# An S5 state-space layer and a feed-forward layer, mixed by a gate: paired 64-row remainders, D·x of odd tokens on GpSimd, one rotation of PSUM banks

## The chip, the cores and the metric

One core of one Trainium2 chip. The time is device microseconds (us) of one launch, as the median of several runs; a run of this kernel differs from the next by up to about 1.6%. "Span" is the time from the first to the last instruction in the one profiled run; it is 1.7 to 2.0 us shorter than that run's launch. The engines are TensorE (PE in the profile, its weight loads PEld), VectorE (DVE), ScalarE (ACT), GpSimd (POOL) and SyncE (SP), which here only issues transfers.

## The reference, cut to what matters

```python
# x: [1, 2048, 448]; P = D = 448; F = 1792; all inputs bf16
g = sigmoid((x * gate_w).sum(-1, keepdims=True))         # one gate per token
# A: a diagonal linear recurrence over the 2048 tokens, complex state of 448
h_t = Lam_bar * h_{t-1} + B_bar @ x_t
a   = 2 * real(C @ h_t) + x * Dskip                      # "D*x" below is x * Dskip
# B: feed-forward
b   = silu(x @ w1) @ w2                                  # 448 -> 1792 -> 448
out = g * a + (1 - g) * b
```

The kernel treats tokens as 1024 pairs. Even and odd tokens go through FFN1 (x @ w1) and FFN2 (@ w2) as separate chunks of 512 tokens, so there are four chunks: two even ones, then two odd ones. The recurrence is run over pairs, with tables of sines and cosines that ScalarE makes (`tables`), a projection on TensorE (`bu`), scans on VectorE (`scan`), combinations of C on VectorE (`side_C`, giving CO and CE), and at the end the y tiles on TensorE (`ytile`). `k0` is the small product of C and B that the even y tiles need.

## The kernel before: the parts that matter

A helper records every operation with the buffers that it reads and writes, and puts in the waits. An operation on an engine thus waits for the last writer of what it reads and for the readers of what it overwrites.

FFN1 contracts over 448 rows, which is three and a half blocks of 128. The half block is padded with zeros to 128 rows, so a block of 128 hidden units costs four matmuls of 512 columns:

```python
BK_F1 = [0, 1, 2, 3]              # PSUM banks of FFN1
BK_F2 = BK_S = [4, 5, 6, 7]       # PSUM banks of everything else

def ffn1(c, fb, ...):             # c: chunk, fb: one of 14 blocks of hidden units
    ...
    for j in range(4):
        ins = pe.matmul(ps[:, bank, :], W[:, j, fb*128:(fb+1)*128],
                        XT[:, j0 + j, h*512:(h+1)*512], start=(j == 0), stop=(j == 3))
    ...
    act: AT[:, fb, :] = Silu(ps[:, bank, :])
```

In an even y tile D·x is folded into `k0`. In an odd one it is four small matmuls with diagonal matrices DO:

```python
def ytile(kt, odd):
    for m in range(7):
        pe.matmul(ps[:, bank, 0:D], HS[:, m, o0:o0+128], C[:, m, :], start=(m == 0), stop=False)
    if odd:
        ...                       # four matmuls of 64 or 128 columns with DO
    else:
        ...                       # four matmuls with KT (from k0)
    dve: out = ps * GT1 + bs(tile)          # g * a + (1-g) * b
```

The gates, on VectorE, read x in its natural layout (XN, which lies where the odd w1 goes later):

```python
def gate():
    for t in range(16):
        dve: JK = XN[:, t*D:(t+1)*D] * GWB, Z[:, t] = row sums    # two SBUF inputs
    ...
    act: GT0 = Tanh(0.5 * Z)
    dve: GT1, GT2 = 0.5 +- 0.5 * GT0
    sp:  load odd w1 into the place of XN
```

The order of the program from the middle on is: gates' sums, `bu` of the first states, `scan(0)`, more `bu`, Tanh, the rest of the scans, FFN2 of chunk 0, FFN1 of chunk 2, FFN2 of 1, C combinations, FFN1 of 3, FFN2 of 2, `k0`, then FFN2 of 3 between y tiles.

Of the kernel before, what the change touches and what calls it, by code (L numbers as in the profile page):

```python
# [10 lines left out]
F32 = DT.float32  # L11
# [133 lines left out]
def gated_mix(nc, A_x, A_Lambda_re, A_Lambda_im, A_B_re, A_B_im, A_C_re, A_C_im, A_log_dt,  # L145
              A_Dskip, B_x, B_w1, B_w2, gate_w, out):
    with ExitStack() as ctx:
# [22 lines left out]
        DO = sb("DO", [128, 4, 128], BF16)  # L170
# [13 lines left out]
        R = sb("R", [3, 512], BF16)  # L184
        RD = sb("RD", [2, 512], BF16)
        PV = sb("PV", [128, 4, 5], F32)
# [5 lines left out]

        LTF = LT[:, :, :, :].rearrange("p a b c -> p (a b c)")
# [5 lines left out]
        BK_F1 = [0, 1, 2, 3]  # L199
        BK_F2 = BK_S = [4, 5, 6, 7]  # L200
# [8 lines left out]

        T.op("dve", lambda e: e.memset(Q1[:, 0, 0:512], 0.0), writes=["Q10"])  # L210
# [3 lines left out]
        T.op("pool", lambda e: e.memset(RD[:, :], 0.0), writes=["RD0", "RD1"])  # L214
        gR, gRD, gB = T.group(), T.group(), T.group()
# [3 lines left out]

        ld("act", W1E[:, 0:3, 0:384], B_w1[0:384, 0:384].rearrange("(j p) f -> p j f", p=128), "W1Eb")  # L220
# [4 lines left out]
        ldt(XT[:, 0:4, 0:512], x2[0:512, 0:512], "XTe0")  # L225
        for i, v in enumerate((A_log_dt, A_Lambda_re, A_Lambda_im)):
            ld("sp", R[i:i + 1, 0:D], row(v), f"R{i}", gR)
# [7 lines left out]
        for h in range(2):  # L235
            ldt(XT[:, 4:7, h * 512:(h + 1) * 512], x2[h * 512:(h + 1) * 512, 512:896], f"XTo{h}")
        B_RAW = ["Bre", "Bim"]
# [8 lines left out]
        T.op("pool", lambda e: e.memset(W1E[64:128, 3, :], 0.0), writes=["W1Ez"])  # L246
# [3 lines left out]
        T.op("pool", lambda e: e.memset(KT[64:128, 3, :], 0.0), writes=["KTz"])  # L250
        SGN = ["SGa", "SGb"]
# [3 lines left out]
        n_f1 = [0]  # L255
        n_f2 = n_s = [0]

        def nxt(banks, n):
            b = banks[n[0] % len(banks)]
            n[0] += 1  # L260
            return b

        def ffn1(c, fb, mm_only=False, act_only=None):
            odd, h = c // 2, c % 2
            bank = nxt(BK_F1, n_f1) if act_only is None else act_only
            W, j0 = (W1O, 3) if odd else (W1E, 0)
            a = AT[c % 2]
            wk = (["W1Oa", "W1Ob", "W1Oz"] if odd else
                  ["W1Ez", "W1Ea", "W1Eb" if fb < 3 else "W1Ec" if fb < 7 else "W1Ed"])
            xk = [f"XTe{h}", f"XTo{h}"] if odd else [f"XTe{h}"]  # L270

            def mm(pe):
                ins = None
                for j in range(4):
                    ins = pe.matmul(ps[:, bank, :], W[:, j, fb * 128:(fb + 1) * 128],  # L275
                                    XT[:, j0 + j, h * 512:(h + 1) * 512],
                                    start=(j == 0), stop=(j == 3))
                return ins
            if act_only is None:
                T.op("pe", mm, reads=wk + xk, writes=[f"ps{bank}"])  # L280
            if mm_only:
                return bank
            T.op("act", lambda e: e.activation(a[:, fb, :], ps[:, bank, :], AF.Silu),  # L283
                 reads=[f"ps{bank}"], writes=[f"AT{c % 2}_{fb}"])

        T.op("dve", lambda e: e.tensor_copy(R[:, D:512], R[:, 384:448]), reads=["R0", "R1", "R2"],
             writes=["Rd"])

        def mm_cols(pe):
            ins = None  # L290
            for pt in range(4):
                ins = pe.matmul(ps[:, 6, pt * 8:pt * 8 + 3], R[0:3, pt * 128:(pt + 1) * 128],
                                ID[0:3, 0:3], start=True, stop=True)
            return ins
        def warm(n):
# [7 lines left out]
        warm(10)  # L303
        first = [ffn1(0, fb, mm_only=True) for fb in range(2)]
        T.op("pe", mm_cols, reads=["R0", "R1", "R2", "Rd", "ID"], writes=["ps6"])
        T.op("dve", lambda e: e.tensor_copy(
            PV[:, :, 0:3], ps[:, 6, 0:32].rearrange("p (t c) -> p t c", c=8)[:, :, 0:3]),
            reads=["ps6"], writes=["PV"])

# [61 lines left out]
        def phase(pt):  # L371
            return HS[:, 2 * pt:2 * pt + 2, :].rearrange("p a b -> p (a b)")[:, 0:2 * NK].bitcast(F32)

        def phases(pt):
            f2 = "f2s" if pt == 3 else "f2"
            X, RR = phase(pt), G[:, 1, :]
            T.op("dve", lambda e: e.tensor_scalar(X, IOTA[:, :], c1(f2, pt), None, ALU.mult),
# [6 lines left out]
        def tables(pt):  # L384
            X = phase(pt)
            T.op("act", lambda e: e.activation(SIN[:, pt, :], X, AF.Sin, scale=SIN_SCALE),
                 reads=[f"F{pt}"], writes=[f"SIN{pt}"])
            yield
            T.op("act", lambda e: e.activation(X, X, AF.Abs), reads=[f"F{pt}"], writes=[f"F{pt}"])
            yield  # L390
            T.op("act", lambda e: e.activation(COS[:, pt, :], X, AF.Sin, bias=HP[:, 0:1],
                                               scale=-SIN_SCALE),
                 reads=[f"F{pt}", "HP"], writes=[f"COS{pt}"])
            T.op("pool", lambda e: e.memset(HS[:, 2 * pt:2 * pt + 2, 0:8], 0.0),
                 writes=[f"F{pt}", f"HSz{pt}"])
            yield
# [96 lines left out]
        def side_diag():  # L493
            def mm(pe):
                ins = None
                for pt in range(4):
                    ins = pe.matmul(ps[:, 7, pt * 8:pt * 8 + 2], RD[0:2, pt * 128:(pt + 1) * 128],
                                    ID[0:2, 0:2], start=True, stop=True)
                return ins
            T.op("pe", mm, reads=["RD0", "RD1", "ID"], writes=["ps7"])  # L500
            T.op("dve", lambda e: e.tensor_copy(
                PV[:, :, 3:5], ps[:, 7, 0:32].rearrange("p (t c) -> p t c", c=8)[:, :, 0:2]),
                reads=["ps7"], writes=["PVD"])
            for j in range(4):
                T.op("dve", lambda e, j=j: e.tensor_scalar(
                    DE[:, j, :], ID[:, :], PV[:, j, 3:4], None, ALU.mult),
                    reads=["ID", "PVD"], writes=[f"DE{j}"])
                T.op("dve", lambda e, j=j: e.tensor_scalar(
                    DO[:, j, :], ID[:, :], PV[:, j, 4:5], None, ALU.mult),
                    reads=["ID", "PVD"], writes=[f"DO{j}"])  # L510
# [4 lines left out]
        def load_xn():  # L515
            ld("sp", XN.rearrange("p (k c) -> p k c", k=NKT), x2.rearrange("(k p) c -> p k c", p=128), "XN")

        def gate():
            for t in range(2 * NKT):
# [4 lines left out]
                if t % 4 == 3:  # L524
# [9 lines left out]
            T.op("pool", lambda e: e.memset(W1O[0:64, 0, :], 0.0), writes=["XN", "W1Oz"])  # L534
            T.dma("sp", lambda e: e.dma_start(W1O[64:128, 0, :], B_w1[0:64, :]), reads=["W1Oz"],
                  writes=["W1Oa"])
            T.dma("sp", lambda e: e.dma_start(
                W1O[:, 1:4, :], B_w1[64:448, :].rearrange("(j p) f -> p j f", p=128)),
                reads=["W1Oz"], writes=["W1Ob"])
# [3 lines left out]
        def ffn2(c, q):  # L543
# [4 lines left out]
            bank = nxt(BK_F2, n_f2)  # L548

            def mm(pe):  # L550
                ins = None
                for fb in range(NFB):
# [7 lines left out]
                 reads=[f"ps{bank}", "GT2"], writes=[f"BS{tile}"])  # L560

        def bu(m, h):
            pt = m // 2
            bank = nxt(BK_S, n_s)
# [12 lines left out]
        def k0(j):  # L577
            bank = nxt(BK_S, n_s)
# [73 lines left out]
        hs_all = [f"HS{m}" for m in range(7)] + [f"HSz{pt}" for pt in range(4)]  # L652

        def ytile(kt, odd):
            tile = 2 * kt + odd
            bank = nxt(BK_S, n_s)
# [4 lines left out]
            def mm(pe):  # L661
                ins = None
                for m in range(7):
                    ins = pe.matmul(ps[:, bank, 0:D], HS[:, m, o0:o0 + 128], C[:, m, :],  # L664
                                    start=(m == 0), stop=False)
                if odd:
                    pe.matmul(ps[:, bank, 0:64], XT[:, 3, t0:t0 + 128], DO[:, 0, 64:128],  # L667
                              start=False, stop=False)
                    for j in range(1, 4):
                        lo = 64 + (j - 1) * 128  # L670
                        ins = pe.matmul(ps[:, bank, lo:lo + 128], XT[:, 3 + j, t0:t0 + 128],  # L671
                                        DO[:, j, :], start=False, stop=(j == 3))
                else:
# [6 lines left out]
                 + [f"KT{j}" for j in range(4)] + ["KTz"] + [f"DO{j}" for j in range(4)],  # L680
# [4 lines left out]
                bs(tile), ALU.mult, ALU.add),  # L685
                reads=[f"ps{bank}", "GT1", f"BS{tile}"], writes=[f"OT{kt % 3}_{odd}"])
# [13 lines left out]
        ld("sp", GWB[:, :], row(gate_w).partition_broadcast(128).rearrange("p o n -> p (o n)"), "GW")  # L700
        load_xn()
# [8 lines left out]
        for fb in range(2):  # L710
            ffn1(0, fb, act_only=first[fb])
        for fb in range(2, NFB):
            ffn1(0, fb)
        tabs = chain(tables(0), tables(3), tables(1), tables(2))
        for fb in range(NFB):
            ffn1(1, fb)
# [3 lines left out]
        run(gates, 5)  # L720
        for h in range(2):
# [6 lines left out]
        bu(6, 1)  # L728
        s3 = scan(3)
# [5 lines left out]
        run(gates)  # L735
# [3 lines left out]
        ld("sp", RD[0:1, 0:D], row(A_Dskip), "RD0", gRD)  # L739
        ld("sp", RD[1:2, 64:512], row(A_Dskip), "RD1", gRD)  # L740
# [9 lines left out]
        for fb in range(NFB):  # L750
            ffn1(2, fb)
# [3 lines left out]
        for fb in range(NFB):  # L755
            ffn1(3, fb)
        for q in range(4):
            ffn2(2, q)
        for j in range(4):
            k0(j)  # L760
        for q in range(4):
            ffn2(3, q)
# [43 lines left out]
```

## Time and profile before

| | before |
|---|---|
| median of the first three runs | 161.76 us |
| span of the profiled run (which took 162.38 us) | 160.6 us |
| TensorE busy | 153.4 us (96%) |
| VectorE busy | 108.6 us (68%) |
| GpSimd busy | 7.3 us (5%) |
| TensorE unbroken | from 14.10 us to 157.5 us |
| last CO piece ready / `k0` starts | 111.39 us / 112.22 us |

From the page of the profile, part 4, the chain of work that ended last, by engine:

```profile
PE 92%; DMA 4%; ACT 2%; DVE 1%; issue 0%
```

TensorE bounds the kernel. But its second is close. These are lines of VectorE's timeline (start in us, duration in us, engine, source line, operation, output<-inputs, sizes, count; in brackets the idle time before it and what ended that): the first gate operations, the first operation of the scans, and the last piece of CO with what follows it. (Here and below the read of the accumulator after each gate operation, 0.08 us, is left out.)

```profile
41.23 0.62 DVE L520 SCALAR_TENSOR_TENSOR JK<-W1O,GWB 128x448 bf16<-128x448 bf16 x1 [7.67 <-DMA W1O<-in_A_x_dram]
41.78 0.62 DVE L520 SCALAR_TENSOR_TENSOR JK<-W1O,GWB 128x448 bf16<-128x448 bf16 x1
...
49.97 0.69 DVE L602 TENSOR_TENSOR Q<-HS,COS 128x1024 bf16<-128x1024 bf16 x1
...
110.79 0.68 DVE L411 SCALAR_TENSOR_TENSOR CO<-XC,P,TMP 128x448 bf16<-128x448 bf16 x1
111.39 0.45 DVE L408 TENSOR_SCALAR TMP<-XC,P 128x448 f32<-128x448 bf16 x1
```

From start to start a gate operation takes 0.55 us, sixteen of them 8.74 us (41.23 to 49.97). From 41.23 us on VectorE has no gap that counts until the last CE piece at 118.2 us. And this is TensorE around `k0`, where CO is first needed:

```profile
101.63 10.76 PE L553 MATMUL ps<-W,AT 128*128 128x448 bf16 x56
112.22 1.49 PE L584 MATMUL ps<-CO,BB 128*128 128x448 bf16 x7
...
116.31 0.22 PE L586 MATMUL ps<-DE,ID 128*128 128x128 bf16 x1
116.46 1.51 PE L584 MATMUL ps<-CO,BB 128*64 128x448 bf16 x7
117.81 0.19 PE L586 MATMUL ps<-DE,ID 128*64 128x64 bf16 x1
117.93 2.25 PE L553 MATMUL ps<-W,AT 128*128 128x448 bf16 x11
```

CO is there only 0.8 us before TensorE wants it.

### The profile page before, as it was taken

Reading aid. Unit: us, or ns where it says so; the run is one execution under the profiler, and the core shown is the slowest. Engines: PE = TensorE matmul, PEld = TensorE weight load, DVE = VectorE, ACT = ScalarE, POOL = GpSimd, SP = SyncE. Lnnn points to the kernel's source line nnn. Section 1 sums busy time; section 2 is a strip of 40 time slices with the busy share of each in tenths; the row PEclk is TensorE's granted clock in tenths of the full one; section 3 lists DMA queues with packets and bytes.
Section 4 is the critical chain, followed back from the end, with each engine's and each line's share of the span. In section 5 each row is a group of like instructions: output and inputs, shape, how many; then the busy total and the mean of one; then the engine's idle time right before and its main releaser. Section 6 shows DMA issues by size and latency. Waiting matters only on the chain.

```text
span 160.6 us, 2016 instructions
## 1 busy us (share of the span) xinstructions
PE 153.4 (96%) x772; PEld 73.8 (46%) x772; DVE 108.6 (68%) x216; ACT 67.7 (42%) x111; POOL 7.3 (5%) x16
## 2 busy tenths in 40 slices
PE   6696999999999999999999999999999999999992
PEld 2132444444444455444455444455555555555551
DVE  0027999930799999999999999999941131133341
ACT  3019769999587610766522476331421101100000
POOL 7500000000003000000000000000000000000000
PEclk9999999999999999999999999999999999999999
DMA  5996979799930730026930000000000100102211
GB/s 109 297 354 142 213 142 119 121 149 395 323 82 4 255 145 0 0 63 107 116 69 0 0 0 0 4 2 0 0 0 0 61 30 27 57 0 88 87 57 57
DMA packets 26787, 14.76 MB, mean 92 GB/s; under 512 B 19861, under 2 KB 26010, under 8 KB 26778
## 3 DMA queue, kind: packets, MB, share of 16 engines
q1 hardware_dynamic: 25498, 13.03, 34.3%
q10 hardware_dynamic: 1280, 1.61, 3.3%
q8 instruction: 6, 0.10, 0.2%
q14 instruction: 3, 0.02, 0.0%
HBM read 7.92 MB, written 1.84 MB: 61 GB/s over the span
## 4 chain that ended last, share of the span: by engine, by line
PE 92%; DMA 4%; ACT 2%; DVE 1%; issue 0%
PE ps L275 30%; PE ps L553 26%; PE ps L664 13%; PE ps L569 13%; DMA XT<-in_A_x_dram 4%; PE ps L675 4%; PE ps L584 3%; PE ps L671 1%; ACT L340 1%; ACT P L334 0%; DVE OT L683 0%; ACT AT L283 0%; PE ps L667 0%; ACT JK L340 0%; PE ps L586 0%
## 5 line engine op out<-in xcount | busy, mean ns | idle before, releaser
L553 PE MATMUL ps<-W,AT 128*128 128x448 bf16 x224 | 43.5, 353 | 0.0
L283 ACT ACTIVATE AT<-ps 128x512 bf16<-128x512 f32 x56 | 32.5, 596 | 10.6 <-PE ps L275 10.3
L553 PEld LDWEIGHTS ps<-W,AT 128*128 128x128 bf16 x224 | 21.7, 98 | 20.1 <-issue 0.2
L683 DVE SCALAR_TENSOR_TENSOR OT<-ps,GT,LT 128x448 bf16<-128x448 f32 x16 | 10.9, 684 | 29.0 <-PE ps L675 22.3
L275 PE MATMUL ps<-XT,W1E 128*128 128x512 bf16 x112 | 26.4, 397 | 2.8 <-DMA XT<-in_A_x_dram 1.4
L558 ACT ACTIVATE LT<-ps,GT 128x448 bf16<-128x448 f32 x16 | 9.9, 634 | 43.6 <-PE ps L553 35.3
L275 PE MATMUL ps<-XT,W1O 128*128 128x512 bf16 x112 | 24.5, 379 | 0.0
L569 PE MATMUL ps<-XT,LT 128*128 128x512 bf16 x98 | 21.3, 379 | 0.0
L275 PEld LDWEIGHTS ps<-XT,W1E 128*128 128x128 bf16 x112 | 11.1, 101 | 17.6 <-POOL KT L250 2.3
L275 PEld LDWEIGHTS ps<-XT,W1O 128*128 128x128 bf16 x112 | 10.9, 98 | 12.9
L605 DVE TENSOR_TENSOR_SCAN G<-P,Q 128x1024 f32<-128x1024 f32 x7 | 15.7, 2276 | 0.0
L569 PEld LDWEIGHTS ps<-XT,LT 128*128 128x128 bf16 x98 | 9.6, 98 | 11.6
L520 DVE SCALAR_TENSOR_TENSOR JK<-W1O,GWB 128x448 bf16<-128x448 bf16 x16 | 8.8, 621 | 7.7 <-DMA W1O<-in_A_x_dram 7.7
L664 PE MATMUL ps<-CE,HS 128*128 128x448 bf16 x56 | 11.9, 353 | 0.0
L664 PE MATMUL ps<-CO,HS 128*128 128x448 bf16 x56 | 11.9, 352 | 0.0
L573 ACT ACTIVATE HS<-ps 128x512 bf16<-128x512 f32 x14 | 8.2, 596 | 5.1 <-PE ps L569 4.5
L602 DVE TENSOR_TENSOR Q<-G,SIN 128x1024 bf16<-128x1024 f32 x7 | 8.5, 1219 | 0.0
L602 DVE TENSOR_TENSOR Q<-G,COS 128x1024 bf16<-128x1024 f32 x7 | 8.5, 1210 | 0.0
L664 PEld LDWEIGHTS ps<-CO,HS 128*128 128x128 bf16 x56 | 5.5, 98 | 5.1
L675 PE MATMUL ps<-KT,XT 128*128 128x448 bf16 x32 | 7.4, 352 | 0.0
L664 PEld LDWEIGHTS ps<-CE,HS 128*128 128x128 bf16 x56 | 5.3, 98 | 4.4
L584 PE MATMUL ps<-CO,BB 128*128 128x448 bf16 (+1 forms) x28 | 5.7, 353 | 0.0
(75 smaller groups left out, 110.5 us busy)
## 6 DMA issues: line engine op xcount, KB each, us to landing
W1O<-in_A_x_dram SPq DMA_DIRECT2D x1, 1792.0 KB, 10.3
out_dram<-OT SPq DMA_DIRECT2D x8, 224.0 KB, 1.9
W<-in_B_w_dram SPq DMA_DIRECT2D x1, 1568.0 KB, 13.8
W1O<-in_B_w_dram SPq DMA_DIRECT2D x1, 1344.0 KB, 6.3
W1E<-in_B_w_dram ACTq DMA_DIRECT2D x1, 672.0 KB, 7.8
W1E<-in_B_w_dram ACTq DMA_DIRECT2D x1, 384.0 KB, 6.3
BB<-in_A_B_re_dram SPq DMA_DIRECT2D x1, 336.0 KB, 6.4
BB<-in_A_B_im_dram SPq DMA_DIRECT2D x1, 336.0 KB, 6.9
```

What stands on the lines that cost most here:

```text
L275: ins = pe.matmul(ps[:, bank, :], W[:, j, fb * 128:(fb + 1) * 128], XT[:, j0 + j, h * 512:(h + 1) * 512], start=(j == 0), stop=(j == 3))
L283: T.op("act", lambda e: e.activation(a[:, fb, :], ps[:, bank, :], AF.Silu), reads=[f"ps{bank}"], writes=[f"AT{c % 2}_{fb}"])
L520: T.op("dve", lambda e, t=t: e.scalar_tensor_tensor(JK[:, t % 2, :], XN[:, t * D:(t + 1) * D], 1.0, GWB[:, :], ALU.mult, ALU.mult, accum_o ...
L553: ins = pe.matmul(ps[:, bank, 0:D], a[:, fb, q * 128:(q + 1) * 128], W2[:, fb, :], start=(fb == 0), stop=(fb == NFB - 1))
L558: T.op("act", lambda e: e.activation(bs(tile), ps[:, bank, 0:D], AF.Copy, scale=GT[:, 2, tile:tile + 1]), reads=[f"ps{bank}", "GT2"], writ ...
L569: ins = pe.matmul(ps[:, bank, :], LT[:, m, j, :], XT[:, j, h * 512:(h + 1) * 512], start=(j == 0), stop=(j == 6))
L584: ins = pe.matmul(ps[0:M, bank, 0:D], BB[:, m, D + j * 128:D + j * 128 + M], CO[:, m, :], start=(m == 0), stop=False)
L602: T.op("dve", lambda e: e.tensor_tensor(o, a, b, op), reads=reads, writes=writes)
L605: T.op("dve", lambda e: e.tensor_tensor_scan(G[:, c, :], rb, Q1[:, c, :], 0.0, ALU.mult, ALU.add), reads=[f"Q1{c}", "rr"], writes=[f"G{c}"])
L664: ins = pe.matmul(ps[:, bank, 0:D], HS[:, m, o0:o0 + 128], C[:, m, :], start=(m == 0), stop=False)
L675: ins = pe.matmul(ps[:, bank, 0:D], XT[:, j, t0:t0 + 128], KT[:, j, :], start=False, stop=(j == 3))
L683: T.op("dve", lambda e: e.scalar_tensor_tensor(o[:, odd * D:(odd + 1) * D], ps[:, bank, 0:D], GT[:, 1, tile:tile + 1], bs(tile), ALU.mult, ...
```

## The change

Its intent is to take work from TensorE. Two 64-row remainders of FFN1 go to the two halves of the array and run at once, so the time of seven of fourteen remainder matmuls per chunk is saved (in the first chunk five, since its first four blocks are not paired). D·x of odd tokens leaves TensorE for GpSimd, which is idle. All eight PSUM banks are one rotation, so FFN1 may run eight blocks ahead of ScalarE. Dskip comes as a fourth parameter row, so no small matmul is needed later to turn it into a column. The warm-up grows from 10 to 14 matmuls. With these comes some reordering: the gates' Tanh earlier, and half of FFN2's last chunk before `k0`. The diff, cut to its core:

```diff
-        BK_F1 = [0, 1, 2, 3]
-        BK_F2 = BK_S = [4, 5, 6, 7]
+        BANKS = list(range(8))
...
+        def ffn1_mm(c, fbs, single=False):           # fbs: up to four blocks
...
+            for fb, bank in zip(fbs, banks):
+                    for j in range(3):                # the three full row blocks
+                        ins = pe.matmul(ps[:, bank, :], W[:, w0 + j, ...], XT[:, x0 + j, hs],
+                                        start=(j == 0), stop=False)
+            def rest(pe):                             # the 64-row remainders, alternating halves
+                for i, (fb, bank) in enumerate(zip(fbs, banks)):
+                    up = (i % 2 == 1 and not single) != bool(odd)
+                    p = slice(64, 128) if up else slice(0, 64)
+                    x = XT[p, 3, hs] if up == bool(odd) else XR[p, hs]
+                    ins = pe.matmul(ps[:, bank, :], W[p, jr, ...], x, start=False, stop=True)
...
+        def skip():                                   # right after the gates' sums
+            for kt in range(NKT):
+                pool: PD[:, kt, :] = XN[:, t*D:(t+1)*D] * DBC        # fp32 <- bf16, bf16
+        def skip_gated():                             # after GT1
+            for kt in range(NKT):
+                pool: PD[:, kt, :] = PD[:, kt, :] * GT1[t]           # fp32
...
+            if odd:                                   # in ffn2
+                pool: PD[:, kt, :] = PD[:, kt, :] + bs(tile)
...
-                if odd:                               # in ytile: four matmuls with DO
...
-        warm(10)
+        warm(14)
...
         bu(6, 1)
+        run(gates)                                    # Tanh, GT1, GT2, load of odd w1
         s3 = scan(3)
...
             bu(2, h)
             bu(3, h)
-        run(gates)
...
         for q in range(4):
             ffn2(2, q)
+        for q in range(2):
+            ffn2(3, q)
         for j in range(4):
             k0(j)
+        for q in range(2, 4):
+            ffn2(3, q)
```

XR is a copy of the half block of x on the other 64 partitions, made by small transfers. The place of the even w1, free after the even chunks, holds PD.

## The prediction

It was written with the kernel before and its profile at hand, and nothing of the change built or run.

> **What bounds the kernel now.** TensorE. In the chain of waits it has 92% of the 160.6 us span; in the timeline it runs back to back from 14.10 to 157.5 us, at 216 ns per 512-column matmul (56 in 12.09 us) and 189 ns per 448-column one (56 in 10.59). Before 14.10 it first waits for the first transposed x (7.0 us), runs eight FFN1 matmuls at half pace (446 ns each), then 1.4 us for the first SiLU, with all four FFN1 banks full. After it come 0.68 us of VectorE and the last store (about 3.1 us together). VectorE is close behind: its timeline is unbroken from 41.2 us (x landed) to the last CO piece at 111.4 and the last CE piece at 118.2; TensorE needs them at 112.4 (k0) and 120.75 (even y tiles).
>
> **What the change does to TensorE.**
> - Pairing: 52 of 56 remainders run as 26 pairs; if a pair really costs one matmul, 26 x 0.216 = -5.6 us.
> - Switching: the Trainium skill, "TensorEngine Tiling (Array Packing)", Key Properties, says that changing the tiling mode drains the array. The trace agrees: k0's fourth block (64 columns) starts and ends with about 0.09 to 0.10 us extra (0.15 and 0.12 us from the short matmul's start to the next, against 0.06 between full blocks). 16 groups x 2 x 0.1 = +3.2 us, a little of it hidden at the start. Net FFN1 gain only about 2.5 us: a full chunk goes from 12.1 to about 11.4 us.
> - D*x of odd tokens: 8 x 0.20 = -1.6 us; the Dskip columns -0.3 us.
> - Start: longer warm-up keeps the array busy until x lands, so the first eight matmuls run near full pace (up to -1.7 us); eight banks take 8 blocks ahead of the first SiLU instead of 4. Together about -2.5 us.
> TensorE alone: about -7 us, span about 153.6.
>
> **What it adds.** GpSimd gets 24 operations of 128x448. I estimate about 1 us per two-input one (its 128x1024 cast takes 1.04 us): 8 multiplies beside VectorE's 16 gate operations (8.8 us), 8 scalings beside the scans, 8 additions beside the C combinations. The skill, "SBUF — State Buffer", Who interferes with whom, says that a VectorE instruction with two SBUF inputs contends with a GpSimd one that reads SBUF. No GpSimd arithmetic overlaps VectorE there in this trace, so its size is open; I estimate VectorE's chain 4 us later (0 to 12). VectorE saves about 0.9 us (no DO pieces). The reordering of FFN2 before k0 gives CO 5.3 us more room, but TensorE is 7 us faster: k0 would start near 112.4, CO is ready at 110.5 + delay. So about 2 of 4 us delay reach the critical path: span about 155. The W1O reload now waits for eight GpSimd multiplies; expect it to land near 60 to 63 us, just in time for odd FFN1 (about 63).
>
> **Prediction.** 156 us (span plus about 1.1), range 152.5 to 160.5. Faster by over 2% 0.75, within 2% 0.18, slower 0.07.
>
> **What shows it.** Right: odd FFN1 chunks of 11.2 to 11.6 us; each four remainders about 0.43 us plus two gaps of 0.1; FFN1 of both even chunks done near 31.5 us instead of 35.0; no D*x matmuls; TensorE stalls, if any, before k0 waiting for CO, and gate operations longer than 0.55 us beside GpSimd.
>
> **What would make it wrong.** Remainders that don't overlap (chunk 12.5 us or more); GpSimd blocking VectorE for whole instructions, so that gates, scans and C combinations slip by over 8 us (no gain, or a loss); late XR copies or W1O; no contention at all (153 to 154 us).

## The result

| | before | after |
|---|---|---|
| median | 161.69 us (161.2 to 163.71, 4 runs) | 170.91 us (170.41 to 171.09, 4 runs) |
| ratio, 95% interval | | 1.0576 (1.0538 to 1.0614) |
| span of the profiled run | 160.6 us | 168.8 us |
| TensorE busy | 153.4 us | 152.8 us (91%) |
| VectorE busy | 108.6 us | 121.8 us (72%) |
| GpSimd busy | 7.3 us | 40.2 us (24%) |
| last CO piece ready / `k0` starts | 111.39 / 112.22 us | 125.34 / 125.57 us |

The changed kernel is 5.8% slower. A ratio is the mean time of one kernel's fast runs over that of the other's fast runs of the same rounds, so it is not quite the ratio of the medians. Of the four runs of the kernel before in this table, one (163.71 us) is over 1.5% above the fastest and so counts as slow; the ratio given is the one without it.

The chain of work that ended last now belongs to VectorE (the page of the changed kernel, part 4):

```profile
DVE 60%; PE 24%; DMA 9%; SPq 3%; ACT 1%; issue 1%
```

VectorE's timeline at the same three places (the gate operations are now L554, the scans L639, CO L440):

```profile
42.00 0.63 DVE L554 SCALAR_TENSOR_TENSOR JK<-W1O,GWB 128x448 bf16<-128x448 bf16 x1 [8.94 <-DMA W1O<-in_A_x_dram]
42.55 1.45 DVE L554 SCALAR_TENSOR_TENSOR JK<-W1O,GWB 128x448 bf16<-128x448 bf16 x1
43.93 1.44 DVE L554 SCALAR_TENSOR_TENSOR JK<-W1O,GWB 128x448 bf16<-128x448 bf16 x1
...
57.37 0.68 DVE L639 TENSOR_TENSOR Q<-HS,COS 128x1024 bf16<-128x1024 bf16 x1
...
124.74 0.68 DVE L440 SCALAR_TENSOR_TENSOR CO<-XC,P,TMP 128x448 bf16<-128x448 bf16 x1
125.34 0.81 DVE L437 TENSOR_SCALAR TMP<-XC,P 128x448 f32<-128x448 bf16 x2
```

The first gate operation takes 0.55 us from start to start, the next ones 1.38 us, as long as GpSimd's eight multiplies last. GpSimd's timeline in that stretch:

```profile
42.05 11.08 POOL L539 TENSOR_TENSOR W1E<-W1O,DBC 128x448 f32<-128x448 bf16 x8 [37.80 <-DMA W1O<-in_A_x_dram]
```

Eight multiplies in 11.08 us are 1.39 us each. GpSimd's begin at 42.05, 43.60, 44.97 us and so on, the gate operations at 42.55, 43.93, 45.30: the two engines took turns, one operation of each. After the eight, the gate operations are back at 0.55 us.

TensorE stands still twice (its timeline, and after it the list of waits of TensorE, with total, number and longest wait in us):

```profile
49.80 3.40 PE L606 MATMUL ps<-XT,LT 128*128 128x512 bf16 x15
59.82 12.86 PE L587 MATMUL ps<-W,AT 128*128 128x448 bf16 x56 [6.62 <-ACT HS L610]
72.52 2.75 PE L282 MATMUL ps<-XT,W1O 128*128 128x512 bf16 x12
...
125.57 2.77 PE L621 MATMUL ps<-CO,BB 128*128 128x448 bf16 x7 [3.56 <-DVE CO L440]
```

```profile
PE ps L587 <- ACT HS L610: 6.6, 1, 6.6
PE ps L621 <- DVE CO L440: 3.6, 1, 3.6
```

The first stall, before FFN2, is at the end of a short chain. ScalarE's timeline shows it:

```profile
41.15 0.60 ACT L610 ACTIVATE HS<-ps 128x512 bf16<-128x512 f32 x1
57.47 0.22 ACT L562 ACTIVATE GT<-Z 128x16 f32<-128x16 f32 x1 [15.72 <-DVE JK L554]
57.60 1.13 ACT L422 ACTIVATE COS<-HS,HP 128x1024 bf16<-128x1024 f32 x1
59.17 1.08 ACT L610 ACTIVATE HS<-ps 128x512 bf16<-128x512 f32 x2 [0.44 <-ACT COS L422]
```

The Tanh of the gates (L562) was moved ahead of the last tables and of the evictions of `bu` in ScalarE's queue. It waits for the slowed gates until 57.47 us, and behind it wait evictions that would free PSUM banks. TensorE fills the eight banks and stops. After the stall it also runs slowly: FFN2 of chunk 0 takes 12.70 us (59.82 to 72.52) where 56 such matmuls take 10.69 without it (78.67 to 89.36 in the kernel before). The windows view (start:end, length, busy times of PE, PEld, DVE, ACT and POOL, then PEclk, the TensorE clock granted, then DMA) gives the reason; the granted clock falls in the stall and is 0.66 of full speed on average in the 6 us after it (asked in finer windows, it is 0.50 from 58 to 64 us):

```profile
53.00:60.00 7.00, 0.38 (x2) 0.13 (x2) 6.96 (x21) 2.08 (x4) 0.13 (x1) 0.80 0.18 46
60.00:66.00 6.00, 6.00 (x22) 2.65 (x21) 5.96 (x5) 5.88 (x10) 0.00 (x0) 0.66 0.92 272
```

This is what the Trainium skill, "TensorE: Matmul & The Clock Gate", Part 1, describes: an idle array gets half its clock, and sustained work gets it back. The same happens at `k0`, which takes 7.35 us (125.57 to 132.92, at a granted clock of 0.77) instead of 5.71 (112.22 to 117.93 before).

The two stalls and the slow matmuls after them make 6.62 + 2.0 + 3.56 + 1.6 = 13.8 us. Without them the span would be about 155 us. So TensorE's own work did shrink about as intended. An odd FFN1 chunk takes 11.41 us now (72.52 to 83.93, against 12.09 before), and an even and an odd y tile together 3.40 us instead of 3.60.

VectorE's delay at CO adds up like this, from the starts in its timeline:

| stretch of VectorE | before | after | longer by |
|---|---|---|---|
| x has landed | at 41.23 | at 42.00 | 0.8 |
| sixteen gate operations | 8.74 | 15.37 | 6.6 |
| scans and what lies between | 53.09 | 57.37 | 4.3 |
| diagonal matrices | 1.50 | 1.43 | -0.1 |
| CO combinations | 6.83 | 9.17 | 2.3 |
| CO ready | 111.39 | 125.34 | 14.0 |

GpSimd was at work in each of the stretches that grew: the multiplies in the gates, the scalings in the scans, the additions in the last scan and the combinations. The row of the diagonal matrices hides the same: it lost five of its nine operations and is hardly shorter, as the four left took 1.51 us where eight such had taken about 1.3.

### The profile page after: what moved, and what is told of

The parts are those of the page before. It is cut to its first block, busy times and chain, and to the rows that moved or that the text cites. A ratio compares the mean times of both kernels' runs of the same rounds, so it can differ in the third digit from the quotient of the medians.

```text
span 168.8 us, 1989 instructions
## 1 busy us (share of the span) xinstructions
PE 152.8 (91%) x740; PEld 68.4 (41%) x740; DVE 121.8 (72%) x211; ACT 63.2 (37%) x111; POOL 40.2 (24%) x34
## 4 chain that ended last, share of the span: by engine, by line
DVE 60%; PE 24%; DMA 9%; SPq 3%; ACT 1%; issue 1%
DVE Q L639 18%; PE ps L701 13%; DVE G L642 9%; DVE JK L554 9%; DMA W1O<-in_A_x_dram 6%; PE ps L621 4%; DVE HS L639 4%; PE ps L705 4%; DVE TMP L437 4%; DVE CO L440 3%; DMA R<-in_A_Dskip_dram 3%; PE ps L587 3%; DVE BB L440 3%; DVE HS L412 2%; DVE P L359 2%; SPq L204 2%
## 5 line engine op out<-in xcount | busy, mean ns | idle before, releaser
L304 ACT ACTIVATE AT<-ps 128x512 bf16<-128x512 f32 x56 | 29.0, 609 | 12.8 <-PE ps L294 12.8
L554 DVE SCALAR_TENSOR_TENSOR JK<-W1O,GWB 128x448 bf16<-128x448 bf16 x16 | 15.4, 1028 | 8.9 <-DMA W1O<-in_A_x_dram 8.9
L546 POOL TENSOR_SCALAR W1E<-W1E,GT 128x448 f32<-128x448 f32 x8 | 16.4, 2047 | 19.5 <-DVE GT L566 18.7
L282 PE MATMUL ps<-XT,W1E 128*128 128x512 bf16 x84 | 19.7, 380 | 0.9 <-DMA XT<-in_A_x_dram 0.9
L596 POOL TENSOR_TENSOR W1E<-W1E,LT 128x448 f32<-128x448 f32 x8 | 10.0, 1249 | 41.2 <-ACT LT L592 41.2
L539 POOL TENSOR_TENSOR W1E<-W1O,DBC 128x448 f32<-128x448 bf16 x8 | 10.5, 1316 | 38.3 <-DMA W1O<-in_A_x_dram 37.8
L282 PE MATMUL ps<-XT,W1O 128*128 128x512 bf16 x84 | 19.5, 380 | 0.0
L713 DVE SCALAR_TENSOR_TENSOR OT<-ps,GT,LT 128x448 bf16<-128x448 f32 x8 | 5.5, 683 | 18.0 <-PE ps L705 18.0
L282 PEld LDWEIGHTS ps<-XT,W1E 128*128 128x128 bf16 x84 | 7.5, 98 | 11.9 <-issue 2.9
L713 DVE SCALAR_TENSOR_TENSOR OT<-ps,GT,W1E 128x448 bf16<-128x448 f32 x8 | 5.5, 684 | 5.1 <-PE ps L701 5.1
L639 DVE TENSOR_TENSOR Q<-G,SIN 128x1024 bf16<-128x1024 f32 x7 | 8.8, 1253 | 0.0
L639 DVE TENSOR_TENSOR Q<-G,COS 128x1024 bf16<-128x1024 f32 x7 | 8.4, 1207 | 0.0
(76 smaller groups left out, 154.9 us busy)
## 6 DMA issues: line engine op xcount, KB each, us to landing
W<-in_B_w_dram SPq DMA_DIRECT2D x1, 1568.0 KB, 13.9
```

The costliest lines, as they stand in the source:

```text
L282: ins = pe.matmul(ps[:, bank, :], W[:, w0 + j, fb * 128:(fb + 1) * 128], XT[:, x0 + j, hs], start=(j == 0), stop=False)
L304: T.op("act", lambda e: e.activation(a[:, fb, :], ps[:, bank, :], AF.Silu), reads=[f"ps{bank}"], writes=[f"AT{c % 2}_{fb}"])
L539: T.op("pool", lambda e, t=t, kt=kt: e.tensor_tensor(PD[:, kt, :], XN[:, t * D:(t + 1) * D], DBC[:, :], ALU.mult), reads=["XN", "DBC"], wr ...
L546: T.op("pool", lambda e, t=t, kt=kt: e.tensor_scalar(PD[:, kt, :], PD[:, kt, :], GT[:, 1, t:t + 1], None, ALU.mult), reads=[f"PD{kt}", "GT ...
L554: T.op("dve", lambda e, t=t: e.scalar_tensor_tensor(JK[:, t % 2, :], XN[:, t * D:(t + 1) * D], 1.0, GWB[:, :], ALU.mult, ALU.mult, accum_o ...
L639: T.op("dve", lambda e: e.tensor_tensor(o, a, b, op), reads=reads, writes=writes)
```

## The experiments

The theory: GpSimd's arithmetic holds up VectorE, VectorE's chain then ends last, and the rest of the change is sound. The first rival: the loss comes from the new order (Tanh early) and the single rotation of banks, that is from the 6.6 us stall. Twelve kernels were run, in three sets. The result is right in all but one (noted there).

### First set: undo the GpSimd part, undo the order, undo both, and keep GpSimd busy without reading

**D·x back on TensorE.** The GpSimd operations go, and the DO matmuls return. Their Dskip column, shifted by 64, is made as in the kernel before, by a tiny matmul in mid-stream, now on a bank of the one rotation.

```diff
+            bank = nxt()                # in side_diag, after FFN2 of chunk 1
+            pe: ps[:, bank, ...] = RD[0:1, ...].T @ ID[0:1, 0:1]
+            dve: PVD = ps[:, bank, ...]
-        skip(); skip_gated(); the additions in ffn2
```

> The changed kernel with D*x of odd tokens back on TensorE (no GpSimd arithmetic at all, no D broadcast); all else as changed. Theory (GpSimd's SBUF reads slow VectorE, and VectorE's chain is what ends last): gate operations back to 0.55 us each (15.4 to 8.8 us in all), last CO piece near 112 us instead of 125.4, TensorE unbroken from FFN2 into k0, span about 156.5 us, time about 157.5 us, 3% faster than the kernel before. Rival (the loss comes from the new order, that is gates before the later tables on ScalarE, and the one PSUM rotation): FFN2 still stalls several us before its first block and time stays above 162 us.

Measured: 174.26 us, ratio 1.0748 (1.0694 to 1.0801): slower than the changed kernel. The gate operations were back at 0.55 us and CO was ready at 111.74 us, as the theory had it. The stall before FFN2 was gone too, with Tanh still early. But my edit had made a new stall. TensorE in this run:

```profile
88.89 2.12 PE L284 MATMUL ps<-XT,W1O 128*128 128x512 bf16 x9
103.62 0.61 PE L284 MATMUL ps<-XT,W1O 128*128 128x512 bf16 x1 [12.62 <-DVE PVD L533]
```

The tiny matmul takes one bank of the rotation at 85.5 us. The copy that frees it stands in VectorE's queue behind two scans, until 103.41 us. Eight allocations later the rotation comes back to that bank, and TensorE waits 12.6 us. In the kernel before, such a matmul was harmless, since FFN1 had banks of its own. So the fourth parameter row of the change is not just tidier: with a single rotation of banks, a small result whose reader comes late stops everything. The run tells nothing against either theory as to the loss, so it was mended in the second set.

**Tanh back in its old place.** GpSimd's work stays.

```diff
         bu(6, 1)
-        run(gates)
...
             bu(3, h)
+        run(gates)
         run(s3, 1)
```

> The changed kernel with only the gates' Tanh put back to its old place in program order (after the evictions that feed scans 3 and 1); GpSimd arithmetic kept. Theory (VectorE's chain is the limit and swallows the 6.6 us stall of FFN2 and its cold clock): the stall before FFN2 goes, TensorE then waits about 12 us before k0 instead of 3.6, last CO piece still at 124 to 126 us, time 169 to 171 us. Rival (the stall of FFN2 itself is the loss): its 6.6 us plus the 2.2 us at low clock come back, time 161 to 163 us.

Measured: 171.69 us, ratio 1.0603 (1.0544 to 1.0663). The stall before FFN2 is gone and nothing is won. CO was ready at 125.06 us, and TensorE waited for it 4.5 us before `k0`, not the 12 us that I had expected. It had already waited 3.1 us for the odd w1, whose load is issued only when the slowed gates and multiplies are done (at 58.27 us here, at 58.66 in the changed kernel, where the stall hid it), and 1.9 us for banks of FFN2; and matmuls were slow after each wait. This falls against the rival: the 6.6 us stall alone is not the loss, because VectorE's chain ends at the same time with or without it.

**Both undone.** The edit is the two above together.

> Both undone. Theory: with gates fast again Tanh comes near 51 us, before TensorE runs out of PSUM banks, so its place in the order costs nothing: within 0.5% of the run with D*x on TensorE alone, about 157.5 us. Rival (order matters by itself): 1.5% or more faster than that run.

Measured: 173.52 us, ratio 1.0703 (1.0643 to 1.0764), with the same stall of TensorE as in the first run of this set (13.4 us). It says nothing about order beyond that; it was repeated in the second set without the bad bank.

**GpSimd writes only.** Each GpSimd operation becomes a memset of 3 or 5 blocks of 448 fp32, with the same waits. Its output is wrong, which doesn't matter for the time.

```diff
-  pool: PD[:, kt, :] = XN[...] * DBC
+  pool: PD[:, a:a+3, :] = 0.0
-  pool: PD[:, kt, :] = PD[:, kt, :] * GT1[t]
+  pool: PD[:, a:a+5, :] = 0.0
-  pool: PD[:, kt, :] = PD[:, kt, :] + bs(tile)
+  pool: PD[:, a:a+3, :] = 0.0
```

> The changed kernel with each of the 24 GpSimd operations replaced by one memset that takes about as long (3, 5 and 3 blocks of 448 fp32), same waits, same places: GpSimd still busy and still writing SBUF but reading none of it. The result is wrong on purpose. Theory (VectorE is held by GpSimd's reads of SBUF): gate operations back at 0.55 us, CO ready near 112 us, span about 154.6 us, time about 155.7 us. Rival (any GpSimd activity, its writes included, or the added waits hold VectorE): gate operations still over 0.9 us, time above 162 us.

Measured: 164.41 us, ratio 1.0148 (1.0104 to 1.0191), between the two expectations. VectorE beside the memsets of the first group, and GpSimd:

```profile
43.56 0.62 DVE L558 SCALAR_TENSOR_TENSOR JK<-W1O,GWB 128x448 bf16<-128x448 bf16 x1
44.11 0.62 DVE L558 SCALAR_TENSOR_TENSOR JK<-W1O,GWB 128x448 bf16<-128x448 bf16 x1
```

```profile
43.03 10.16 POOL L540 MEMSET W1E<- 128x1344 f32 x8 [38.77 <-DMA W1O<-in_A_x_dram]
```

The gate operations take 0.55 us from start to start although GpSimd is just as busy. So what held them was its reading. But another kind of VectorE operation is held by writes. A TENSOR_SCALAR of four elements per partition, which took 0.16 us in the kernel before, takes 1.53 us beside a memset here, and the other TENSOR_SCALARs beside memsets grew too, while operations with two inputs did not:

```profile
72.78 1.53 DVE L356 TENSOR_SCALAR P<-P 128x4 f32<-128x4 f32 x1
```

The Trainium skill, "SBUF — State Buffer", Who interferes with whom, says both: VectorE's operations with two SBUF inputs contend with GpSimd instructions that read SBUF, not with those that only write; and `tensor_scalar` can enter a mode that uses the second pair of ports, and can then contend with any GpSimd instruction on them. The trace agrees on both counts, though it does not show the mode. I had expected only the first; the second is why CO came at 119.46 us here and not near 112 (1.7 us of the difference is x, which landed later in this run: the first gate operation is at 43.01 us, against 41.30 in the run with five rows below).

### Second set: the clean undo, and the parts of TensorE's gain

**D·x on TensorE, second Dskip column as a fifth parameter row.** No matmul in mid-stream any more.

```diff
-        R = sb("R", [4, 512], BF16)
+        R = sb("R", [5, 512], BF16)
+        ld("sp", R[4:5, 64:512], row(A_Dskip), "R4", gR)
-  the tiny matmul and the copy in side_diag
+  dve: DO[:, j, :] = ID * PV[:, j, 4:5]
```

> The run with D*x on TensorE again, but its second Dskip column now comes with the first parameters (a fifth row), so no small matmul in mid-stream holds one of the eight PSUM banks until VectorE gets to it (that held TensorE 12.6 us there). Theory (the loss of the change is GpSimd's hold on VectorE; nothing else in it costs): no stall after 14 us, k0 near 112.8 us with CO ready near 111.6, span about 155.8 us, time about 157 us, 3% faster than the kernel before. Rival (the single PSUM rotation, the order of gates, or the switching of the array cost too): TensorE still stalls several us and time is 160 us or more.

Measured: 157.72 us, ratio 0.9772 (0.9726 to 0.9818), span 155.7 us. After the start TensorE waits for nothing; CO is ready at 111.45 us and `k0` starts at 112.55. The last CO piece, the first matmuls of `k0`, and the chain that ended last, of this run:

```profile
110.84 0.68 DVE L441 SCALAR_TENSOR_TENSOR CO<-XC,P,TMP 128x448 bf16<-128x448 bf16 x1
112.55 1.49 PE L607 MATMUL ps<-CO,BB 128*128 128x448 bf16 x7
...
PE 92%; DMA 3%; POOL 1%; SPq 1%; issue 1%; DVE 0%; POOLq 0%
```

With GpSimd's arithmetic taken out, and everything else of the change kept, the kernel is 2.3% faster than the one before instead of 5.8% slower. This is the main result.

**The same, Tanh in its old place.**

> The same with the gates back at their old place in program order. Theory: with fast gates the place matters little, within 1% of the run with five rows, at most 1 us slower where the first odd FFN1 waits for W1O or the banks of FFN2. Rival (the early gates block ScalarE whatever their speed): 1.5% or more faster than that run.

Measured: 158.06 us, ratio 0.9796 (0.9738 to 0.9854), the same span of 155.7 us. The intervals of this run and the last overlap widely. So the early Tanh costs nothing where the gates are fast.

**No pairs.** All remainders on one half of the array.

```diff
-                    up = (i % 2 == 1 and not single) != bool(odd)
+                    up = bool(odd)
```

> The run with five rows, but all 64-row remainders on the same half of the array, so no two of them can overlap. Theory (pairs overlap fully, and each switch of the array's mode costs about 0.1 us): 26 x 0.216 = 5.6 us slower than the run with five rows, odd FFN1 chunks 12.9 us instead of 11.4 and so longer than the 12.1 of the kernel before. Rival (the gain of FFN1 comes from elsewhere, as from the PSUM banks): less than 2 us slower.

Measured: 163.35 us, ratio 1.0114 (1.007 to 1.0157), that is 5.63 us longer than with pairs. The remainders of one group of four, first without pairs (one line for four matmuls, one after the other), then with pairs in the run with five rows:

```profile
68.77 1.03 PE L295 MATMUL ps<-XT,W1O 64*128 64x512 bf16 x4
69.73 2.76 PE L283 MATMUL ps<-XT,W1O 128*128 128x512 bf16 x12
```

```profile
65.90 0.39 PE L295 MATMUL ps<-XT,W1O 64*128 64x512 bf16 x1
65.91 0.39 PE L295 MATMUL ps<-XR,W1O 64*128 64x512 bf16 x1
66.13 0.38 PE L295 MATMUL ps<-XT,W1O 64*128 64x512 bf16 x1
66.13 0.38 PE L295 MATMUL ps<-XR,W1O 64*128 64x512 bf16 x1
66.44 2.76 PE L283 MATMUL ps<-XT,W1O 128*128 128x512 bf16 x12
```

The two of a pair start within 10 ns of each other. The next full matmul starts 0.96 us after the first remainder without pairs and 0.54 us with them. An odd chunk takes 12.92 us without pairs (66.08 to 79.00): worse than the zero padding of the kernel before (12.09), because the switching of the array stays and its reward is gone.

**Groups of six.** Remainders are collected over 6, 6 and 2 blocks instead of 4, 4, 4 and 2.

```diff
-            for f in range(f0, NFB, 4):
-                for fb, bank in ffn1_mm(c, list(range(f, min(f + 4, NFB)))):
+            for f in range(f0, NFB, 6):
+                for fb, bank in ffn1_mm(c, list(range(f, min(f + 6, NFB)))):
```

> The run with five rows, remainders collected over six blocks instead of four: 6+6+2 instead of 4+4+4+2, one pair of mode switches less per full chunk. Theory (a switch costs about 0.1 us): each odd chunk 0.2 us shorter (11.2 us), time 0.5 to 0.8 us shorter if VectorE's CO (near 111.6 us) doesn't hold k0, else within 0.3 us of the run with five rows. Rival (the cost sits in the remainders themselves): chunks unchanged at 11.4 us.

Measured: 156.97 us, ratio 0.9726 (0.9677 to 0.9775), span 154.9 us. An odd chunk takes 11.20 us (62.92 to 74.12) instead of 11.41: 0.21 us for one group less, so about 0.1 us per switch. This is the fastest version that I found: 2.7% faster than the kernel before.

### Third set: the warm-up, and the GpSimd groups one by one

This set ran on another chip than the second; the kernel before took 162.34 us beside it, against 161.4 there. Small differences between the sets are not read.

**Warm-up of 10 matmuls**, in the version with groups of six (`warm(14)` becomes `warm(10)`).

> The run with groups of six, but with the old warm-up of 10 matmuls. Theory (the longer warm-up keeps TensorE busy until x lands, so that its clock is up for the first eight FFN1 matmuls): these eight take 446 ns each as before instead of about 216, the first parameters' matmul comes near 10.7 us instead of 9.8, time about 1 us longer than the run with groups of six (about 158.0 us). Rival (the warm-up changes nothing): within 0.3 us of it.

Measured: 157.23 us, ratio 0.9661 (0.9598 to 0.9723), against 156.97 us with 14 (in another set, with other runs of the kernel before beside it). The first FFN1 matmuls ran at full pace in spite of the short warm-up. The kernel before, and this run, both with a warm-up of 10:

```profile
7.13 3.57 PE L275 MATMUL ps<-XT,W1E 128*128 128x512 bf16 x8 [1.43 <-DMA XT<-in_A_x_dram]
```

```profile
7.12 1.46 PE L283 MATMUL ps<-XT,W1E 128*128 128x512 bf16 x6 [1.42 <-DMA XT<-in_A_x_dram]
8.51 0.60 PE L295 MATMUL ps<-XT,W1E 64*128 64x512 bf16 x2
```

So the number of warm-up matmuls did not decide it alone, for both had the same warm-up and the same pause of 1.4 us after it. What did, the clock records in the runs' traces show (the windows view prints 1.00 before the first record and so hides it). The rise to full clock is recorded at 10.59 us in the profile of the kernel before and at 6.25 us here, and in both the matmuls start about 427 ns apart before that moment and about 216 ns apart after it. The Trainium skill, "TensorE: Matmul & The Clock Gate", Part 1, says that the clock is judged in windows that don't start with the kernel, so that the moment of the rise varies from run to run. The records agree: in every profile of this case, what lies between two changes of the clock is a whole multiple of 3.413 us. Count back by that from the rise: TensorE was busy for 84% of the stretch before it here (2.84 to 6.25 us). In the kernel before it was busy for 58% of the stretch from 3.76 to 7.17 us, and the clock rose one stretch later. So a warm-up of 10 was late there and in time here by where the windows fell. My theory is neither borne out nor refuted: in all twelve profiles with a warm-up of 14 the clock rose before x landed, by 6.64 us (in the memset run it fell again for one stretch, from 9.66 us, after a pause of 2.1 us), but two profiles with 10 are too few to set against them.

**Only the multiplies.** To the version with five rows, the eight GpSimd multiplies are added, their result used by nothing.

```diff
+        def skip():  pool: PD[:, kt, :] = XN[:, t*D:(t+1)*D] * DBC
         run(gates, 5)
+        skip()
```

> The run with five rows (D*x on TensorE), with only the eight GpSimd multiplies of the change added beside the gates, their result used by nothing. Theory: gate operations beside them 1.38 us, the sixteen 15.4 us instead of 8.8, CO ready near 118.1 us instead of 111.4, TensorE waits about 5.5 us before k0 and runs some matmuls at low clock after; time 163 to 165 us. Rival (the later GpSimd groups do the harm): under 159 us.

Measured: 167.45 us (165.97 to 167.61; the profiled run is the 165.97), ratio 1.029 (1.021 to 1.0369). The gate operations took 1.38 us beside the multiplies, and CO was ready at 117.55 us, near the 118.1 expected. But TensorE did not wait for CO. It lost its time earlier:

```profile
PE ps L585 <- ACT HS L605: 5.6, 1, 5.6
```

That is the stall before FFN2 again, through the early Tanh, and slow matmuls after it. `k0` started at 121.07 us, 8.5 us later than with five rows alone, and by then CO was there. The loss was larger than the 163 to 165 us that I had expected, and its place was not the one that I had named. So slow gates have two ways to cost time: through Tanh in ScalarE's queue, and through VectorE's own chain. Here the first was the longer one.

**The same multiplies on another tile.** Both inputs are the small tile DBC.

```diff
-  pool: PD[:, kt, :] = XN[:, t*D:(t+1)*D] * DBC
+  pool: PD[:, kt, :] = DBC * DBC
```

> The same eight multiplies, but both inputs are the small tile with D, not the tile with x that the gate operations read. Theory (VectorE and GpSimd share a way into SBUF, whatever they read): as the run before, gate operations 1.38 us, 163 to 165 us. Rival (they collide because they read the same tile): gate operations 0.55 us, about 157.7 us.

Measured: 165.62 us, ratio 1.0179 (1.0102 to 1.0257). VectorE:

```profile
43.19 1.35 DVE L553 SCALAR_TENSOR_TENSOR JK<-W1O,GWB 128x448 bf16<-128x448 bf16 x1
44.47 1.34 DVE L553 SCALAR_TENSOR_TENSOR JK<-W1O,GWB 128x448 bf16<-128x448 bf16 x1
```

They take 1.28 us from start to start, nearly as before. So it is not the tile with x that the two collide on.

**Only the scalings and the additions.** To the version with five rows, without the multiplies.

> The run with five rows, with only the eight scalings and the eight additions of the change on GpSimd, their result used by nothing. Theory (the delays of VectorE add up): CO ready 7 to 8 us later than in the run with five rows (near 119 us), of it about 5 during the scans of the scalings and 2.4 beside the C combinations; TensorE waits about 6 us before k0; time 163 to 165 us. Rival (only the multiplies do harm, scalings and additions fit between): under 159 us.

Measured: 166.1 us, ratio 1.0198 (1.0129 to 1.0267). The time is a little above the 163 to 165 us expected. CO was ready at 118.44 us (near 119 expected), 7.0 us later than with five rows alone, and this time the wait was where the theory had it:

```profile
PE ps L619 <- DVE CO L442: 5.5, 1, 5.5
```

The multiplies alone delay CO by 6.1 us (111.45 to 117.55), the scalings and additions alone by 7.0 us. Together that is 13.1 us, and the changed kernel had 13.9 us over the version with five rows (125.34 less 111.45). Counted from the moment that x landed in each run, it is 6.4 and 6.4 us, together 12.9, against 13.2. The delays of VectorE add up. One thing went the other way here: a GpSimd addition that began at 111.23 us took 6.79 us, while VectorE ran all CO combinations but the last at their usual pace. And in the changed kernel a scan that began at 74.02 us took its usual 2.29 us, while a scaling that began at 74.31 took 3.20 us (the shortest took 1.40). Either engine can be the one that is held.

## Why the prediction was wrong

- **What bounds the kernel before.** Right: TensorE, with VectorE's CO less than 1 us behind.
- **Pairing and switching.** Right. I estimated 5.6 us for the pairs (5.63 measured by undoing them), 0.1 us per switch (0.21 us per pair of switches measured), and an odd chunk of about 11.4 us (11.41 measured). The switching cost was read from a place in the kernel before that has nothing to do with FFN1: the fourth block of `k0`.
- **D·x off TensorE.** Right: 0.20 us per odd tile.
- **The start.** The sum was about right: both even chunks were done at 31.88 us, against 31.5 foreseen and 34.83 before. But part of that is luck: in the one profile of the kernel before the clock rose late, at 10.59 us, and the run with 10 shows that it can rise at 6.25 us with the short warm-up too. That the longer warm-up did it, as I had written, is not shown.
- **TensorE alone: span about 153.6 us.** Right within about 2 us: taking the stalls and their slow matmuls out of the changed kernel's span leaves about 155. The run with five rows, which keeps the 1.6 us of D·x on TensorE, has 155.7. (From span to launch the prediction added 1.1 us; in the runs it is 1.7 to 2.0.)
- **"I estimate VectorE's chain 4 us later (0 to 12)." This is the step that failed.** It was 14.0 us: CO, reckoned for 110.5 us plus the delay, came at 125.34. The mechanism had been named, with its source, and listed among what could go wrong ("GpSimd blocking VectorE for whole instructions"), but its size was mis-set. The case that I wrote down as a risk was the actual one. The gates alone took 6.6 us more, since eight of the sixteen operations took 1.38 us each and not 0.55; scans and combinations added 4.3 and 2.3 us. The prediction gave no split of its 4 us, so which group it had too small can't be said. It set about 1 us for a two-input GpSimd operation and had no figure for the scalings; these took 2.1 us (eight in 17.13 us in the run with scalings and additions only). The 0.9 us that it gave VectorE for the missing DO pieces shrank to 0.1, for the four left ran slower.
- **"About 2 of 4 us delay reach the critical path."** The slack behind it was right: `k0` could start at 112.55 us without GpSimd, CO was ready at 111.45. All of the delay beyond the first microsecond or so then reached `k0`, and that is what a chain with 1 us of slack has to do.
- **What the prediction does not have**: the early Tanh in ScalarE's queue. It looked for stalls of TensorE only before `k0`. With fast gates the move is harmless; with slow gates it stopped TensorE for 6.6 us. In the changed kernel that stall was hidden behind the wait for CO (undoing it alone won nothing), but with the multiplies alone it was the loss. That both would have to be undone separately if only the multiplies were kept is argued from the traces; no run tried the multiplies with Tanh late.
- **The odd w1.** Expected to land near 60 to 63 us and be just in time. Its large part was issued at 58.66 us and took 9.0 us, so it landed near 67.7 us. It would have been late, and was so by 3.1 us in the run with Tanh late; in the changed kernel the earlier stall hid it.

## What to carry to other kernels

An idle engine is not a free one: before moving work to GpSimd, look at which VectorE operations will run beside it, and, as these runs have it, plan with the two as one engine wherever VectorE has two SBUF inputs or runs a TENSOR_SCALAR in SBUF. When the second-longest chain has less than 1 us of slack, cost the change on that chain first, and take the worst case of a contention as the case to plan with until a run says otherwise. When several engines share one rotation of buffers or one in-order queue, an item whose input may come late (a Tanh, a tiny matmul's result) must stand where nobody urgent is behind it.

## What the Trainium skill lacked or had wrong

- "SBUF — State Buffer", Who interferes with whom: its rule calls the shared pair of ports an exclusive lock, but it spells out blocking for a whole instruction only for the 2-port modes, and gives no size for a VectorE operation with two SBUF inputs beside a reading GpSimd. Here such operations took turns: 0.55 us became 1.38 us per 128x448 operation (1.28 with another tile), and one GpSimd addition was held for 6.79 us.
- "TensorEngine Tiling (Array Packing)", Key Properties: changing the mode drains the array, without a figure. Here about 0.1 us per change, 0.21 us per pair.
- "GPSIMD Engine Reference", 4.1 Engine selection: it calls one-input work "roughly line-rate" and two-input work the slow kind. Here a scaling of a 128x448 fp32 tile by one scalar per partition took 2.1 us on average (1.40 at the least), an addition of a bf16 tile to such a tile 1.03 us when VectorE was quiet. The scalings never ran beside a quiet VectorE, so their time alone stays open.
- "TensorE: Matmul & The Clock Gate", Part 1: it says that what is issued after the first 3.4 us or so runs at full clock, and warns that the moment varies from run to run. It doesn't say which share of a window must be busy. Here, with 4.45 us of warm-up and a 1.4 us pause, the clock rose at 10.59 us in one profile and at 6.25 us in another; a stretch of 3.41 us that was 58% busy did not raise it, one of 79% (2.69 us, in the first run with D·x on TensorE) and one of 84% did.
